# Attention and a two-layer MLP in one kernel: two batches share the second layer, with a second level of seven products, and the slots' small work is placed at 14 points

## The chip, the core and the metric

The kernel runs on one core of a Trainium2 chip. The core has five engines, each with its own in-order queue of instructions: TensorE (PE; its weight loads are shown apart as PEld), VectorE (DVE), ScalarE (ACT), GpSimd (POOL) and SyncE (SP, which issues the DMAs here). They wait for one another by semaphores only. The metric is the device time of one execution in microseconds.

## The reference: what is computed

For 8 batches of 12 heads, with 448 positions and a head size of 64, all in float32:

```python
q_n, k_n = rmsnorm(q, g_q), rmsnorm(k, g_k)
scores = q_n @ k_n.T / sqrt(64)
attn = softmax(scores) @ v
x = attn.transpose(0, 2, 1, 3).reshape(8 * 448, 768)
h = x @ w_in                 # 768 x 2048, float64 as given
out = (h - tanh(h)) @ w_out  # 2048 x 768
```

## The kernel before, in words

**Slots.** Attention is done for one pair of heads at a time. There are 48 such steps (8 batches of 6 pairs), numbered s = 0 to 47, and each has a slot in the instruction order, written by hand. Slots 0 to 5 are attention alone, with the rounding of the weights. In slots 6 to 11 the MLP of batch 0 runs beside the attention of batch 1. From slot 12 on, `slot` (the last of the three slot functions) does the values of step s, the scores of step s + 1 and the norms of step s + 2, and fills the rest with MLP matmuls.

**The MLP as a stream.** `mlp` is a generator that issues one matmul at a time: for each batch `hidden` (first layer and h - tanh h) and `project` (second layer). `run(ns)` draws matmuls from it until their estimated time is spent. `gap_ns` says how much MLP belongs to a slot: from slot 12 on four gaps of (H_NS + O_NS) / 24, drawn as eight halves, so that a batch's whole MLP is spread evenly over six slots. Whatever an evacuation or a sum of the MLP needs is issued by the generator at its place in the order, so it lands in the engines' queues between the attention's own work.

**Seven products.** From batch 1 on both layers are multiplied by a scheme of seven products of half-size blocks (`ORDER`: 1, 5, 6, 2, 3, 7, 4), instead of eight. For it, combinations of the weight blocks are made once and kept in DRAM (`w_in_dram`, `w_out_dram`); they are read back through a ring of six places, each load issued five products ahead (`ring_load`). Combinations of the moving side are made for each batch: `tt` from x in `divide` (lines 709 to 712, on POOL), and `tg` from g in `factors` and `rest` (lines 797 to 799 on DVE and POOL, 831 on POOL). A layer of a batch has 168 matmuls of 128x128 by 128x224: `hidden` has four sets of seven products of six matmuls, `project` three sets of seven products of eight. All are issued in line 750.

**Evacuation.** The products go to three PSUM banks named `mm` in turn; products 2, 3 and 7 are added on top of products 1, 5 and 6 in the same bank. DVE and ACT add them up in SBUF (`use`: lines 804 to 820 for the hidden layer, 867 to 881 for the second one). `shrink` (lines 786, 787) does tanh on ACT and the subtraction on DVE or POOL. Work put in `late["todo"]` is issued after the next product. `store` turns a 128x448 block on DVE (line 845) and issues four DMAs.

**A slot in its order.** First `visit`: 8 score matmuls of the last key chunk of step s + 1 (they read its kT and qT), then the values of step s mixed with the scores of s + 1, each exp on ACT. In it, `divide` copies one bank on ACT (line 687), adds the other on DVE (line 688, the "xT add") and multiplies by the reciprocal sums (line 692). Then come eight stretches of MLP matmuls with this work between them:

```python
add(s+1); square_blocks(s+2)                         # 552, 553; 466 on ACT
norm_blocks(s+2)          # 473, 475 to 477, and 478: pow on POOL
add_last(s+1); fold(s+1)                             # 560; 657, 659
scale_blocks(s+2); gather(s+1, 0)                    # 485; 667 on ACT
turn_blocks(s+2, 0); gather(s+1, 1)                  # 495: qT
turn_blocks(s+2, 1)                                  # 499: kT, 500 on ACT
spread_sums(s+1)                                     # 675 to 680
```

Lines 675 to 680 give the reciprocal sums that line 692 of the next visit multiplies by. The kT of step s + 2 is scaled on ACT (line 500) before the scores of the next visit read it.

Of the kernel before, what the change touches and what calls it, by code (L numbers as in the profile page):

```python
# [13 lines left out]
ALU = mybir.AluOpType  # L14
# [130 lines left out]
def bounded_path(tc, ctx, q, k, v, moe_w_in, moe_w_out, out, g_col, ident, ones, half_ones, neg_half, early):  # L145
# [32 lines left out]
    SETS = CF // 4  # L178
    ORDER = (1, 5, 6, 2, 3, 7, 4)
# [18 lines left out]
    gp = pool("gp", bufs=1)  # L198
    wp_stack = ctx.enter_context(ExitStack())
# [14 lines left out]

    def load(s, names):
        b, hp = steps[s]
        for name in names:
            src = {"q": q, "k": k, "v": v}[name]
            if s == 0 and name != "v":
                t = early[name]  # L220
            else:
                shape = [CP, 2, NCH, D] if name == "q" else [P, NCH, 2, D] if name == "k" else [P, 2, NCH, D]
                t = nat.tile(shape, F32, name=f"{name}_nat", bufs=3 if name == "v" else 2)
                fetch(nc, name, t, src[b, 2 * hp : 2 * hp + 2], in_order(s))
            loaded[name, s] = t
# [8 lines left out]
    BLOCKS = {1: 0, 2: 1, 4: 2, 7: 3, 5: 4, 6: 5, 3: 6}  # L234
    w_out_dram = scratch.tile([P, 7, HC, HF, P], F32, name="w_out")
# [140 lines left out]
    def ring_slot():  # L376
# [4 lines left out]
    ring_steps = [  # L381
        (b, layer, j, p)
        for b in range(1, B)
        for layer, count in ((0, SETS), (1, HC))
        for j in range(count)
        for p in ORDER
    ]
    ring_tiles = {}

    def ring_load(to):  # L390

        for n in range(len(ring_tiles), min(to, len(ring_steps))):
            b, layer, j, p = ring_steps[n]
            t = ring_tiles[ring_steps[n]] = ring_slot()
            if layer == 0:
                assert kept[1] > j
                nc.sync.dma_start(out=t[:, : 2 * HALF], in_=w_in_dram[j, p])
            else:
# [55 lines left out]
    def load_blocks(s):  # L454
        b, hp = steps[s]
        t = loaded["qk", s] = late["blocks"].tile([P, 2, NJ, BL], F32, name="qk_nat", bufs=2)
# [13 lines left out]
    def norm_blocks(s):  # L470

        mine, other = (late["blocks"].tile([P, 2 * NJ], F32, name=name, bufs=2) for name in ("rr_mine", "rr_other"))
        nc.vector.reduce_sum(mine, normed[s].rearrange("p i j d -> p (i j) d"), axis=AX.X)
        for g in range(P // BL):
            nc.vector.tensor_copy(out=other[g * BL : (g + 1) * BL], in_=mine[(g ^ 1) * BL : ((g ^ 1) + 1) * BL])
        nc.vector.tensor_tensor(out=mine, in0=mine, in1=other, op=ALU.add)
        nc.vector.tensor_scalar(out=mine, in0=mine, scalar1=1.0 / D, scalar2=1e-6, op0=ALU.mult, op1=ALU.add)  # L477
        nc.gpsimd.tensor_tensor(  # L478
            out=mine, in0=mine, in1=neg_half[:, :1].to_broadcast([P, 2 * NJ]), op=ALU.pow
        )  # L480
        normed["rr", s] = mine

    def scale_blocks(s):
        n, rr = normed[s], normed.pop(("rr", s))
# [59 lines left out]
    def add(s):  # L544
# [8 lines left out]
        nc.vector.tensor_tensor(out=t, in0=t, in1=p[2], op=ALU.add)  # L553
# [99 lines left out]
    def fold(s):  # L653

        t = sums.pop(s)[0].rearrange("p h s -> p (h s)")
        turned_sum = late["blocks"].tile([P, 2 * S], F32, name="sum_T")
        nc.vector.transpose(out=turned_sum, in_=t)
        part = late["blocks"].tile([P, 2 * NJ], F32, name="sum_32")
# [12 lines left out]
    def spread_sums(s):  # L671
# [5 lines left out]
        wide = late["blocks"].tile([2 * BL, NJ, BL], F32, name="sum_w")  # L677
        nc.vector.tensor_copy(out=wide, in_=total[:, :, None].to_broadcast([2 * BL, NJ, BL]))
        rs = whole[s] = late["blocks"].tile([2 * BL, S], F32, name="rs_T")
        nc.vector.transpose(out=rs, in_=wide.rearrange("p j k -> p (j k)"))  # L680

    def divide(s, av):
        b, hp = steps[s]
        rs = whole.pop(s)
        x = xT[b, hp] = xp.tile([P, S], F32, name="xT")
# [15 lines left out]
        if hp < HC:  # L701
            return
        c = hp - HC
        if c == 0:
            tt[b] = tp.tile([P, 3, HC, HS], F32, name="tt", bufs=1)
        eng = nc.vector if b == 0 and c == HC - 1 else nc.gpsimd
        x11, x12, x21, x22 = (xT[b, r][:, n : n + HS] for r in (c, hp) for n in (0, HS))
        t1, t2, t4 = (tt[b][:, i, c] for i in range(3))
        eng.tensor_tensor(out=t1, in0=x12, in1=x11, op=ALU.subtract)
        eng.tensor_tensor(out=t2, in0=x22, in1=t1, op=ALU.subtract)  # L710
        eng.tensor_tensor(out=x12, in0=x22, in1=x12, op=ALU.subtract)
        eng.tensor_tensor(out=t4, in0=x21, in1=t2, op=ALU.subtract)
# [16 lines left out]
    def products(b, layer, count, width, depth, moving, done_with):  # L729
# [8 lines left out]
        def product(j, p, bank, first):  # L738
# [20 lines left out]
            for fn in now:  # L759
                fn()  # L760

# [9 lines left out]
    def hidden(b):  # L771

        g = late["g"] = gp.tile([P, CF, S], F32, name="gT")
# [675 lines left out]
```

## Time and profile before

| what | value |
| --- | --- |
| median of 3 runs | 1391.6 us (1391.22 to 1391.68) |
| the profiled execution | 1391.42 us, of which its span is 1389.6 us |
| granted TensorE clock, mean | 0.992 |
| hidden layer and second layer, batches 1 to 7 (L750) | 2 records for each matmul, 352 to 354 ns each, overlapping |
| pow on POOL (L478) | 33 times, 4.84 us each |
| PE busy in the stretches of 100 us from 250 to 1250 us | 99.64 to 100.00 us |
| DMA | 249.91 MB, mean 180 GB/s |

The profile has a row for each instruction with its start and length. A group of rows has the same line of code, engine and operation; behind its busy time stands the idle time of the engine just before those instructions, and what ended it. Matmuls are pipelined, so the rate is read from the distance of starts over a stretch, not from the length of one row. In the order of time, a line gives the start, the length, the engine, the line of code, the operation with its output and inputs, and in brackets the idle time before it and what ended that.

### The profile page before, as it was taken

The numbers are of one execution on the slowest core, as the hardware profiler recorded it, in microseconds if no ns is written. First come the engines' busy times: TensorE is split into PE (matmuls) and PEld (weight loads), VectorE is DVE, ScalarE is ACT, GpSimd is POOL, SyncE is SP. The second block draws the span as 40 slices with busy tenths as digits, with TensorE's granted clock in tenths as the row PEclk, the third lists the DMA queues.
The fourth block names the chain that finished last, engine by engine and source line by source line (L and its number), as shares of the span: only waits on it lengthen the run. The fifth ranks groups of instructions, "written<-read, shape, count | busy, mean of one in ns | idle before, by whom it ended". The sixth has DMA issues, their size and how long they took to land.

```text
span 1389.6 us, 29917 instructions
## 1 busy us (share of the span) xinstructions
PE 1354.1 (97%) x11840; PEld 1128.4 (81%) x11840; DVE 941.0 (68%) x1545; ACT 504.7 (36%) x1147; POOL 561.8 (40%) x345
## 2 busy tenths in 40 slices
PE   7989899999999999999999999999999999999997
PEld 3458654478898898899889988988988998899997
DVE  4899888856876788567866668657875677633311
ACT  7856554234322433324332343324333234301100
POOL 4656565223642356225444236323552354402310
PEclk9999999999999999999999999999999999999999
DMA  7888778766666666666657666666567667366663
GB/s 170 187 218 240 249 232 222 206 181 170 177 181 160 177 172 165 176 170 181 178 152 195 177 156 188 172 162 183 165 167 176 181 173 189 100 189 184 191 194 90
DMA packets 367657, 249.91 MB, mean 180 GB/s; under 512 B 281748, under 2 KB 309780, under 8 KB 367508
## 3 DMA queue, kind: packets, MB, share of 16 engines
q1 hardware_dynamic: 367504, 247.90, 66.5%
q8 instruction: 96, 1.57, 0.5%
q14 instruction: 53, 0.43, 0.1%
q10 hardware_dynamic: 4, 0.00, 0.0%
HBM read 214.40 MB, written 33.42 MB: 178 GB/s over the span
## 4 chain that ended last, share of the span: by engine, by line
PE 85%; DMA 6%; DVE 4%; SPq 2%; ACT 1%; issue 1%; POOL 1%; ACTq 0%; DVEq 0%; POOLq 0%
PE mm L750 65%; PE sc L521 8%; PE sc L582 6%; PE mm L915 4%; DMA w_raw<-in_moe_w_in_dram 2%; DMA w_f<-w_out 1%; PE sc L570 1%; DMA gT<-in_moe_w_in_dram 1%; DMA w_raw<-in_moe_w_out_dram 1%; DMA k_nat<-in_k_dram 1%; SPq L272 1%; DVE w_out L82 1%; DVE w_out L79 1%; PE sc L620 1%; DVE w_out L335 0%
## 5 line engine op out<-in xcount | busy, mean ns | idle before, releaser
L750 PE MATMUL mm<-xT,w_f 128*128 128x224 f32 x1392 | 278.5, 354 | 1.7 <-DVE s L806 1.7
L750 PEld LDWEIGHTS mm<-xT,w_f 128*128 128x128 f32 x1392 | 261.3, 190 | 16.0 <-issue 10.2
L750 PEld LDWEIGHTS mm<-gT,w_f 128*128 128x128 f32 x1344 | 252.8, 190 | 12.8 <-issue 12.8
L750 PE MATMUL mm<-gT,w_f 128*128 128x224 f32 x1344 | 263.0, 354 | 0.0
L478 POOL TENSOR_TENSOR rr_mine<-rr_mine,neg_half 128x28 f32<-128x28 f32 x33 | 159.7, 4839 | 218.2 <-DVE rr_mine L477 218.2
L521 PE MATMUL sc<-qT,kT 64*32 64x448 f32 (+1 forms) x3072 | 217.4, 503 | 10.0 <-ACT p_last L527 9.0
L750 PE MATMUL mm<-tt,w_f 128*128 128x224 f32 x1044 | 208.7, 353 | 0.0
L750 PEld LDWEIGHTS mm<-tt,w_f 128*128 128x128 f32 x1044 | 197.0, 190 | 4.4 <-issue 4.4
L787 POOL TENSOR_TENSOR gT<-s,th 128x448 f32<-128x448 f32 x96 | 120.4, 1262 | 197.0 <-ACT th L786 188.2
L750 PE MATMUL mm<-tg,w_f 128*128 128x224 f32 x1008 | 197.5, 352 | 0.0
L750 PEld LDWEIGHTS mm<-tg,w_f 128*128 128x128 f32 x1008 | 190.7, 190 | 0.0
L521 PEld LDWEIGHTS sc<-qT,kT 64*32 64x32 f32 x3072 | 71.1, 107 | 78.5 <-issue 56.2
L688 DVE TENSOR_TENSOR xT<-xT,sc 128x448 f32<-128x448 f32 x35 | 21.7, 621 | 166.5 <-PE sc L521 110.8
L710 POOL TENSOR_TENSOR tt<-xT,tt 128x224 f32<-128x224 f32 x23 | 31.1, 1353 | 234.2 <-DVE xT L692 212.0
L667 ACT COPY sum_g<-sum 32x14 f32<-32x14 f32 x280 | 56.3, 201 | 186.2 <-DVE sum L659 180.5
L582 PE MATMUL sc<-p,v_nat 64*32 64x448 f32 x1120 | 110.5, 536 | 0.0
L786 ACT ACTIVATE th<-s 128x448 f32<-128x448 f32 x96 | 55.2, 575 | 112.7 <-DVE s L812 59.8
L527 ACT ACTIVATE p<-sc 128x448 f32<-128x448 f32 x132 | 71.7, 543 | 51.7 <-PE sc L521 39.1
L915 PE MATMUL mm<-gT,w_out 128*128 128x448 f32 x192 | 75.9, 551 | 0.2 <-POOL w_out L90 0.2
L915 PEld LDWEIGHTS mm<-gT,w_out 128*128 128x128 f32 x192 | 36.3, 193 | 38.3 <-issue 35.8
L582 PEld LDWEIGHTS sc<-p,v_nat 64*32 64x32 f32 x1120 | 40.6, 107 | 31.0 <-issue 31.0
L142 POOL TENSOR_TENSOR rr<-rr,neg_half 112x8 f32<-112x8 f32 (+1 forms) x30 | 49.0, 1660 | 33.7 <-DVE rr L141 33.6
(151 smaller groups left out, 1828.3 us busy)
## 6 DMA issues: line engine op xcount, KB each, us to landing
w_f<-w_in SPq DMA_DIRECT2D x196, 384.0 KB, 3.3
w_f<-w_out SPq DMA_DIRECT2D x147, 512.0 KB, 4.2
w_raw<-in_moe_w_out_dram SPq DMA_DIRECT2D x16, 768.0 KB, 5.2
out_dram<-th SPq DMA_DIRECT2D x192, 56.0 KB, 1.9
w_in<-w_out SPq DMA_DIRECT2D x21, 384.0 KB, 5.9
qk_nat<-in_q_dram SPq DMA_DIRECT2D x132, 56.0 KB, 2.5
qk_nat<-in_k_dram SPq DMA_DIRECT2D x132, 56.0 KB, 2.6
v_nat<-in_v_dram SPq DMA_DIRECT2D x72, 96.0 KB, 3.7
```

Of the source, the lines that this page charges most:

```text
L142: nc.gpsimd.tensor_tensor(out=r, in0=r, in1=neg_half[:rows], op=ALU.pow)
L478: nc.gpsimd.tensor_tensor(out=mine, in0=mine, in1=neg_half[:, :1].to_broadcast([P, 2 * NJ]), op=ALU.pow)
L521: nc.tensor.matmul(tiles[h][i * BL : (i + 1) * BL, :n], lhsT=kT[r, c * P + at : c * P + at + BL], rhs=qT[r, first : first + n], start=True ...
L527: nc.scalar.activation(p[:, h, c if c < 2 else 0, :], tiles[h][:, :n], AF.Exp, scale=1.0 if rr is None else rr[:, 0, 2 * c + h : 2 * c + h ...
L582: nc.tensor.matmul(av[g][i * BL : (i + 1) * BL, :S], lhsT=v_nat[keys, h, c, m * BL : (m + 1) * BL], rhs=p[keys, h], start=first, stop=True ...
L667: nc.scalar.copy(out=acc[h * BL : (h + 1) * BL, g], in_=part[g * BL : (g + 1) * BL, h * NJ : (h + 1) * NJ])
L688: nc.vector.tensor_tensor(out=x, in0=x, in1=av[1][:, :S], op=ALU.add)
L710: eng.tensor_tensor(out=t2, in0=x22, in1=t1, op=ALU.subtract)
L750: nc.tensor.matmul(bank[:, f * HS : (f + 1) * HS], lhsT=w[:, c * width + f, :], rhs=moving[p](c), start=(first and f == 0 and c == 0), sto ...
L786: nc.scalar.activation(th, h, AF.Tanh, bias=0.0, scale=1.0)
L787: eng.tensor_tensor(out=g[:, rows, cols], in0=h, in1=th, op=ALU.subtract)
L915: nc.tensor.matmul(bank[:, :S], lhsT=w_out_row(f, n // HC)[:, n % HC * P : (n % HC + 1) * P], rhs=g[:, f, :], start=(f == 0), stop=(f == C ...
```

## The change

- **Two batches share a second layer.** Batches 0 and 1 stay as they are. From batch 2 on the order is `hidden(b)`, `hidden(b + 1)`, `project_pair(b)`. The pair's second layer is one product of 2048 x 896 (both batches' columns side by side), done by seven outer products whose operands are g of one or the other batch, or sums of both, made in place (`outer_sum`). Each outer product has three blocks of 128 rows. One of them is done plainly by eight matmuls of 448 columns; the other two by a second level of seven products of four matmuls of 224 columns each.
- **Inner sums.** The moving side of the inner products is four sums of 128x896 per outer one (`inner_sum`, buffers `u`), made on POOL one outer product ahead (the first four on DVE).
- **Inner weights.** The combinations of weight blocks for the second level are made once, from the kept outer ones, beside the MLP of batch 1 (`inner_steps`): 14 loads of 512 KB, 28 sums of 128x512 on POOL, 35 stores. One step of it is issued after each product.
- **Combining.** `combine_outer` adds the outer products into two accumulators or into an output block, and stores it.
- **The x sums** (`x_sums`, formerly in `divide`) are issued from batch 2 on at the end of the layer before, all on POOL.
- **`factors` and `tg`** exist for batch 1 only.
- **The slots' work** is put at 14 points at equal distances, in smaller pieces. The reciprocal sums (points 12 and 13) and the turn of kT (point 14, the last) now end the slot.
- **How much MLP a slot holds**: slots 12 to 19 share batch 1's MLP (8 slots); after that, of each twelve slots, eight hold two hidden layers and four hold the paired second layer. The last four slots hold the hidden layer of batch 6; that of batch 7 and the last paired layer follow without attention.

The diff, cut to its core:

```diff
     def hidden(b):
...
+        if b < PAIRED or b % 2 == 0:
+            g = gp.tile([P, CF, S], F32, name="gT")
+        else:
+            g = late["second"].tile([P, CF, S], F32, name="g2")
...
     def divide(s, av):
...
-        eng.tensor_tensor(out=t1, in0=x12, in1=x11, op=ALU.subtract)
...
+        if b < PAIRED and hp >= HC:
+            x_sums(b, (c,), range(4), nc.vector if b == 0 and c == HC - 1 else nc.gpsimd)
...
+    def inner_steps():
...
+            for n, (out, x, y, op) in enumerate(work):
+                yield lambda: nc.gpsimd.tensor_tensor(out=out, in0=x, in1=y, op=op)
+                if n == 0 and i + 1 < len(OUTER):
+                    fetch_outer(i + 1)
+            keep(i, 0, a11)
+            keep(i, 1, block(sums, 0, 2))
+            keep(i, 3, a12)
+            keep(i, 4, block(sums, 2, 2))
+            keep(i, 6, a22)
+            yield lambda: None
...
+    def project_pair(b):
...
+        outer_plan = {
+            3: {0: [(0, 0, V), (0, 1, V), (1, 0, G)], 5: [(0, 2, V), (1, 1, G)], 2: [(0, 3, V)],
+                3: [(1, 2, V)], 4: [(1, 3, V)]},
+            2: {0: [(2, 0, V), (2, 1, V)], 1: [(2, 2, V)], 5: [(2, 3, V)]},
+            6: {1: [(3, 0, G)], 2: [(3, 1, G)]},
+            7: {1: [(3, 2, G)], 2: [(3, 3, G)]},
+        }
+        inner_plan = {5: 0, 6: 1, 7: 2, 4: 3}
+        for i in range(4):
+            inner_sum(OUTER[0], i, V)
...
+        def combine_outer(p, m, y):
+            e, f = acc[:, m], acc2[:, m]
...
+            if p == 2:
+                add(o, y, e)
+                store(b, m, o)
+            elif p == 6:
+                add(e, e, y)
+                add(f, f, e)
+            elif p == 7:
+                add(e, e, y)
+            elif p == 5:
+                add(f, f, y)
+                add(o, y, e)
+                store(b + 1, m, f)
+                store(b + 1, HC + m, o)
+            else:
+                add(o, y, e)
+                store(b, HC + m, o)
...
+        for k, p in enumerate(OUTER):
...
+            bank = mm_bank()
+            yield from matmuls(bank, S, lambda i: w[:, i], [rows(p, f, 1, slice(0, S))[:, 0] for f in range(HF)], True)
+            flush()
+            at(k, 0)
+            late["todo"].append(lambda p=p, v=bank[:, :S]: combine_outer(p, HC - 1, v))
...
+            for i, q in enumerate(ORDER):
...
+                first = q not in (2, 3, 7)
+                bank = banks[q] = mm_bank() if first else banks[{2: 1, 3: 5, 7: 6}[q]]
...
+                yield from matmuls(bank, HS, lambda c: w[:, c], moving, first)
+                flush()
...
+                at(k, q)
...
-        return (H_NS + O_NS) / (4 * NP)
+        if s < 2 * NP + 8:
+            return (H_NS + O_NS + AHEAD_NS) / 32
+        return (H_NS if (s - 2 * NP - 8) % 12 < 8 else PAIR_NS) / 16
...
+        work = (
+            ((following, lambda: add(s + 1, False)), (blocks, lambda: square_blocks(s + 2))),
+            ((following, lambda: add_third(s + 1)),),
+            ((blocks, lambda: norm_blocks(s + 2)), (not blocks, turn_rows)),
+            (
+                (blocks, lambda: meet_blocks(s + 2)), (ahead, lambda: squares(s + 3)),
+                (has(s + 4) and not by_blocks(s + 4), lambda: load(s + 4, "qk")),
+            ),
+            ((following, lambda: add_last(s + 1)), (blocks, lambda: power_blocks(s + 2))),
+            ((folded, lambda: fold(s + 1)),),
+            ((folded, lambda: fold_rest(s + 1)),),
+            ((ahead, lambda: norm(s + 3)), (folded, lambda: gather(s + 1, 0))),
+            ((blocks, lambda: scale_blocks(s + 2)),),
+            ((folded, lambda: gather(s + 1, 1)),),
+            ((blocks, lambda: turn_blocks(s + 2, 0)), (ahead, lambda: norm_q(s + 3))),
+            ((folded, lambda: spread_sums(s + 1)),),
+            ((folded, lambda: turn_sums(s + 1)),),
+            ((blocks, lambda: turn_blocks(s + 2, 1)), (s + 3 == TURNED, lambda: load_blocks(s + 3))),
+        )
+        for point in work:
+            run(4 * gap / (len(work) + 1))
...
```

## The prediction

> **What bounds the kernel now.** I read the busy table first, then the stretches, then the order of time of one slot.
>
> ```profile
> span 1389.6 us, 29917 instructions
> PE 1354.1 (97%) x11840; PEld 1128.4 (81%) x11840; DVE 941.0 (68%) x1545; ACT 504.7 (36%) x1147; POOL 561.8 (40%) x345
> ```
>
> PE is busy 97% of the span. From 250 to 1250 us the stretches of 100 us show 99.6 to 100 us of PE in each, at a granted clock of 1.00. So fewer matmuls help only as far as no other engine is late. The chain of waits repeats one slot (one head pair of attention): 112 records of L750 in 21.38 us. A 128x128 by 128x224 f32 matmul is two records, so one costs 21.38/56 = 0.3818 us. Slots start 26.81 us apart (1128.21 to 1155.00 for one of them), so the attention matmuls of a slot, its **visit**, cost 26.81 - 21.38 = 5.43 us.
>
> DVE at 68% looks free. It isn't: this is VectorE's order of time in one slot whose MLP part is hidden layer.
>
> ```profile
> 1128.21 0.62 DVE L688 TENSOR_TENSOR xT<-xT,sc 128x448 f32<-128x448 f32 x1 [5.48 <-ACT xT L687]
> 1128.87 1.25 DVE L692 TENSOR_TENSOR xT<-xT,rs_T 64x448 f32<-64x448 f32 x2
> ...
> 1135.32 0.19 DVE L476 TENSOR_TENSOR rr_mine<-rr_mine,rr_other 128x28 f32<-128x28 f32 x1
> 1135.55 0.18 DVE L477 TENSOR_SCALAR rr_mine<-rr_mine 128x28 f32<-128x28 f32 x1
> 1135.64 0.62 DVE L816 TENSOR_TENSOR s<-mm,s 128x448 f32<-128x448 f32 x1
> 1136.17 1.26 DVE L560 TENSOR_TENSOR rows<-rows,p_last 64x448 f32<-64x448 f32 x2
> ...
> 1141.41 1.23 DVE L485 TENSOR_TENSOR qk_n<-qk_nat,rr_mine 128x896 f32<-128x896 f32 x1
> 1142.56 1.55 DVE L797 TENSOR_TENSOR tg<-gT 128x448 f32<-128x448 f32 x1
> 1144.22 1.37 DVE L798 TENSOR_TENSOR tg<-gT,tg 128x448 f32<-128x448 f32 x1
> 1145.51 0.63 DVE L495 STREAM_TRANSPOSE qT<-qk_n 128x448 f32<-128x448 f32 x1
> 1146.07 0.58 DVE L806 TENSOR_TENSOR s<-mm,s 128x448 f32<-128x448 f32 x1
> 1146.58 0.62 DVE L499 STREAM_TRANSPOSE kT<-qk_n 128x448 f32<-128x448 f32 x1
> ...
> 1149.14 0.58 DVE L787 TENSOR_TENSOR gT<-mm,th 128x448 f32<-128x448 f32 x1
> 1155.00 0.62 DVE L688 TENSOR_TENSOR xT<-xT,sc 128x448 f32<-128x448 f32 x1 [5.28 <-PE sc L521]
> ```
>
> From the first xT add at 1128.21 to 1149.72 DVE never waits: 21.5 us. Then it sits idle until the next xT add, because its next instruction needs the end of the visit; over the kernel L688 has 166.5 us of idle before it in 35 slots, 4.75 us each. 21.5 + 5.3 is the whole 26.8 us. So a hidden-layer slot is already full on DVE as well as on PE. It costs nothing so far because kT (the last thing that the next visit needs) is turned at 1146.58, with 3 us of other DVE work behind it; ACT scales it from 1147.23 to 1147.90, and the visit begins at 1155.00 - 5.48 = 1149.5.
>
> **The change on PE.** By the listing of both kernels' instruction order, attention and batch 0 keep their matmuls. Second layers of batches 1 to 7 fall from 1176 matmuls of 224 columns to 168 (batch 1) + 588 narrow ones + 168 of 448 columns. A wide one costs two narrow ones: 16 of L915 run from 271.65 to 283.87, 12.22/16 = 0.764 us. So 1176 - (168 + 588 + 336) = 84 units less: 84 x 0.3818 = **32.1 us** gained, if nothing is late. The rest goes by the new division of a slot: 42 units in the slots over hidden layers (20 to 27, 32 to 39, 44 to 47), 77 in the four over a paired second layer (28 to 31, 40 to 43), 42.75 in 12 to 19. PE alone then needs 42 x 0.3818 + 5.43 = 21.47, 34.83 and 21.75 us.
>
> **The new loop.** In the changed order the DVE transposes of the sums (point 13) and of kT (point 14) come last in a slot, and DVE's next instruction after kT is the xT add of the next visit. PE's first score matmul of that visit waits for ACT's kT. So a slot can't be shorter than: visit start to xT add, 5.48 (880.52 to 886.00 in one slot), + all DVE work of the slot, + kT on ACT 0.67 and two hand-overs of 0.04 and about 0.1 (the first read at 875.65 to 875.69, the second an estimate): 5.48 + W + 0.8.
>
> W in a hidden-layer slot. Take the 21.5 us above; L797 and L798 leave (2.95, 1142.56 to 1145.51); seven evacuations of 448 columns instead of nine (0.54 from start to start): 21.5 - 2.95 - 1.08 = 17.5. The second way is from the groups' means. Attention: 1.10 + 1.38 + 2 x 0.64 + 1.06 + 4 x 0.25 + 0.19 + 0.18 + 1.43 + 0.64 + 0.63 + 1.11 + 1.09 + 0.23 + 0.23 + 0.48 + 0.64 + 0.62 + 2 x 0.62 = 14.5; evacuations 7 x 0.61 = 4.3; 18.8, less 0.6 since PSUM adds overlap their forerunner by 0.07. One wait may add: pow on POOL ends 4.89 us after L477 (731.64 to 736.53), and the work now between them is 4.6, so 0.3. W is 17.5 to 18.8; I take 18.2, between a slot with quick two-input adds and the means. The slot becomes 5.48 + 18.2 + 0.8 = 24.5 against PE's 21.47: **3.0 us of new PE stall** where there was none.
>
> Slot by slot, DVE work up to kT from the same means less 0.6:
> - Fourteen plain ones (20-22, 24-26, 32-34, 36-38, 44, 45): 14 x 3.0 = 42.
> - 27 and 39 also hold the four first inner sums (128x896, two SBUF inputs, no such row; as L552 to L553, 1.1 to 1.38 each): W 23.7, 30.0 - 21.47 = 8.5 each, 17.
> - 23 and 35: nine POOL sums of the next batch's x (0.66 or 1.5 us, L709, L710) lie ahead of pow and delay DVE's scaling: 3.0 + 2, twice, 10. Slot 19: 1.5.
> - 13 to 15 still hold batch 1's factors: W 19.2, 19.8, 21.5: 3.8 + 4.4 + 6.1. 17 to 19: W 17.2, 1.7 each. 16: none. Together 19.5.
> - Paired slots: W is 22.5, 28.6, 22.7, 29.9 against 34.83 - 6.3 = 28.5, so only the last is over (1.4). But a bank now has to come free within four matmuls (1.53 us). Following slot 29 in its order: its combine of the 448-wide product lies behind two outer sums and ends some 1.1 us late, the evacuations of products 5 and 6 follow 0.4 and 1.2 late: 2.7. I take 5 per phase of four, 10, and 2 in the last pair, which has no attention beside it.
> - Inner weights, made beside batch 1: 28 POOL sums of 512 (128x448 takes 1.135, L787, so 1.3) and 49 DMAs more on SP's in-order queue, whose stores wait for POOL and whose loads wait for stores. Pow queues behind these sums. No row shows it: 0 if POOL is idle then, up to 16 if every second pow is held 4 us (the landing time of 384 to 512 KB loads, 3.3 to 4.2). I take 5. Behind the stores on SP stand ring loads, five products (11 us) ahead of need.
>
> Stalls: 42 + 17 + 10 + 1.5 + 19.5 + 12 + 5 = 107. Net: -32 + 107 = +75. The profiled execution took 1391.42 (span 1389.6 and 1.8 around it; the median of the runs is 1391.6, the same within 0.2). 1391.4 + 75 = **1466 us**. With W 17.5, no hold by DMA and 4 for the paired slots the stalls are 69 (1428); with W 18.8, 16 there and 30 in the paired slots 153 (1512).
>
> What goes at nothing: ring traffic (a second layer drops from 2 x 21 loads to 35 smaller ones per pair), stores (the same 192), the last store (two adds and a transpose behind the last matmul, 0.7 longer).
>
> On POOL and DVE together the trace shows the same add of 128x896 (L485) at 1.09, mostly 1.54 and up to 2.01 us, and L710 at 0.66 or 1.50. The Trainium skill (SBUF — State Buffer, "Who interferes with whom") says why such times jump: a VectorE instruction with two SBUF inputs and a GpSimd instruction that reads SBUF exclude each other for a whole instruction. It speaks against moving 30 sums per pair to POOL: held up once by each, DVE would lose some 30 x 2.2 us, an estimate by that rule, about 130 us more for the two phases with attention than I count.
>
> **Rivals.**
> 1. *The saving arrives* (faster). One mechanism: the finer points let DVE work through a hidden slot in 21.47 - 6.3 = 15.2 us, so kT is never late; then 1391.4 - 32 + 2 to 4 = 1361 to 1364. For it: the factors and their POOL partners are gone and two-input adds get quicker. Against: the quietest slot of the trace needs 17.5 for the same list.
> 2. *Milder*: W near 17 and clean paired slots, 14 x 1.8 = 25 and 35 elsewhere: 1395 to 1428.
> 3. *POOL becomes the bound*: a paired phase has 30 sums of 896 (2.25 us by 2 x L787's 1.135, 3.0 by L799's 1.52), 4 pows of 4.8 and 12 x sums, 95 to 122 us of 145; slot 29 alone has ten sums, 27 to 35 us of 35. If u sums come late, PE waits 10 us or more a phase: 1512 to 1560.
> 4. *It doesn't do what it says*: excluded nearly, the listing counts the matmuls.
>
> **How the numbers follow.** The DVE loop 0.74; milder 0.08; POOL 0.09; faster 0.07; no change (stalls eat just the gain) 0.02. A change of under 0.2% is about what a measurement of this kernel can't tell from none. Faster 0.07, same 0.02, slower 0.91. The main case alone is 1428 to 1512; half of either neighbour brings the range to 1415 to 1520.
>
> **What would show it.** Right: PE idle of some 3 us once per hidden slot ahead of the scores, released by ACT's kT; slots 24 to 25 us apart there; DVE idle only before the xT add; paired slots 35 to 37.5 us apart; L1023 with 84 units less. Wrong: PE at 99% in those slots with a distance of 21.5 us (rival 1); matmuls that wait for POOL's u (rival 3); pow that waits for DMAs beyond 5 us in all.

## The result, and the profile after

The changed kernel takes 1512.4 us (median of 4 runs, 1511.27 to 1515.54) against 1391.55 (4 runs of the kernel before): 1.088 times as long, 95% interval 1.086 to 1.089. That is 121 us more; 75 were predicted, with 1520 as the upper end of the range.

The page's first part, for the changed kernel:

```profile
span 1511.1 us, 29074 instructions
PE 1358.7 (90%) x11336; PEld 1046.7 (69%) x11336; DVE 1049.5 (69%) x1620; ACT 509.1 (34%) x1159; POOL 735.9 (49%) x415
```

PE has 504 records fewer, two for each matmul: 252 matmuls less. That is the count of the prediction (924 in the second layers of batches 1 to 7 instead of 1176, 168 of them wide; a wide one counted twice, 84 units less). Yet PE's busy time grew by 4.6 us, and its share fell from 97% to 90%. Two things hide in that: idle time, and matmuls that run longer. The list of waits of PE (us in total, times, longest) opens with a row that the kernel before doesn't have:

```profile
PE sc L552 <- ACT kT L531: 85.0, 27, 6.8
```

Here is a plain hidden-layer slot, DVE's order of time with ACT's kT and PE's first score matmul put in. It answers to the slot from 1128.21 to 1155.00 of before.

```profile
515.50 0.62 DVE L736 TENSOR_TENSOR xT<-xT,sc 128x448 f32<-128x448 f32 x1 [8.03 <-PE sc L552]
516.16 1.27 DVE L740 TENSOR_TENSOR xT<-xT,rs_T 64x448 f32<-64x448 f32 x2
...
528.05 1.09 DVE L516 TENSOR_TENSOR qk_n<-qk_nat,rr_mine 128x896 f32<-128x896 f32 x1 [0.85 <-POOL rr_mine L509]
...
532.26 0.62 DVE L725 STREAM_TRANSPOSE rs_T<-sum_w 64x448 f32<-64x448 f32 x1
532.82 0.59 DVE L530 STREAM_TRANSPOSE kT<-qk_n 128x448 f32<-128x448 f32 x1
...
533.45 0.67 ACT L531 ACTIVATE kT<-kT,g_col 128x448 f32<-128x448 f32 x1 [3.10 <-DVE kT L530]
...
534.17 0.61 PE L552 MATMUL sc<-qT,kT 64*32 64x224 f32 x16 [2.65 <-ACT kT L531]
...
539.67 0.62 DVE L736 TENSOR_TENSOR xT<-xT,sc 128x448 f32<-128x448 f32 x1 [6.25 <-PE sc L552]
```

The loop closes as predicted: DVE works without a pause (but for 0.85 us for pow) up to kT, ACT scales kT, PE waits 2.65 us for it, and the next xT add comes 6.25 us after kT. The slot is 24.17 us, where PE alone needs 21.47 by the prediction's count: 17.91 from the xT add to the end of kT (the prediction's W was 18.2), and 6.26 from there to the next xT add.

The distances of the xT adds give the account slot by slot. "Over PE" is the sum of the slots less what PE alone needs (21.47, 21.75 in slots 13 to 19, 34.83 in paired ones).

| slots | distances, us | over PE | predicted |
| --- | --- | --- | --- |
| 14 plain ones | 24.11 to 24.28 | 38 | 42 |
| 27, 39 | 30.53, 30.61 | 18 | 17 |
| 23, 35 | 29.17, 29.24 | 15 | 10 |
| 13 to 19 | 31.19, 33.69, 34.54, 27.23, 24.83, 23.89, 26.73 | 50 | 21, and 5 for the inner weights |
| 28 to 31, 40 to 43 | 37.68, 41.63, 35.51, 42.03; the same within 0.1 | 35 | 10 |

Together 157; less the 32.1 gained on PE, 125, against 121 measured. (The last pair, predicted at 2, has no xT adds to read.) So the named loop is there in its named size. Against the prediction's terms, slots 13 to 19 are 24 us more, the paired ones 25 and slots 23 and 35 5, and the plain ones 4 less: these make up the missing 46 us, but for a few.

**A slow stretch behind the long waits.** In the plain slots the time from the end of kT to the next xT add is 6.2 to 6.3 us. In nine others (13 to 16, 19, 23, 27, 35, 39) it is 8.0 to 9.2, 21 us more in all (they lie within the table's rows), though the same instructions stand there. Slot 23: PE's wait, and busy times by stretch (the span of the stretch, its length, then the busy time of PE, PEld, DVE, ACT and POOL, each with its number of instructions; the number behind POOL's is the granted clock, ahead of the DMA share and GB/s):

```profile
608.83 1.00 PE L552 MATMUL sc<-qT,kT 64*32 64x224 f32 x16 [3.62 <-ACT kT L531]
```

```profile
600.00:605.00 5.00, 4.60 (x24) 4.46 (x24) 4.15 (x7) 2.75 (x10) 3.82 (x2) 1.00 0.55 137
608.83:611.00 2.17, 2.17 (x32) 0.89 (x40) 0.00 (x0) 1.44 (x4) 1.14 (x1) 0.50 0.79 177
611.00:614.00 3.00, 3.00 (x40) 0.88 (x32) 0.00 (x0) 0.54 (x1) 0.00 (x0) 0.50 0.39 155
614.00:615.00 1.00, 1.00 (x24) 0.35 (x16) 0.00 (x0) 0.54 (x1) 0.00 (x0) 0.66 0.00 0
615.00:617.00 2.00, 2.00 (x56) 0.71 (x40) 0.00 (x0) 1.33 (x3) 0.00 (x0) 1.00 0.00 0
```

After 3.62 us without a matmul the clock is 0.50 for over 5 us: the first 16 score matmuls take 1.00 us where those of the plain slot above took 0.61, behind a wait of 2.65. In this run the clock fell behind each wait for kT of 3.28 us or more (the nine slots) and behind none of 2.91 or less, and each of the nine cost 1.7 to 3 us beyond the wait itself. In few_sums (below) it fell behind two of 2.61 and 2.64 us as well (slots 24 and 36, 1.7 us longer than the other plain ones), so the length of the wait alone doesn't decide.

The Trainium skill (TensorE: Matmul & The Clock Gate, Part 1) puts the idle time after which the clock is halved at about 3.4 us, and the busy time that brings it back at the same. The 2.65 and 3.62 us agree with the first; the 3.28, and the 2.61 and 2.64 of few_sums, don't. In slot 23 the clock was back at 1.00 only 5.2 to 6.2 us after PE's restart.

### The profile page after: what moved, and what is told of

Read it like the earlier page. It is cut to its first block, busy times and chain, and to the rows that moved or that the text cites. A ratio compares the mean times of both kernels' runs of the same rounds, so it can differ in the third digit from the quotient of the medians.

```text
span 1511.1 us, 29074 instructions
## 1 busy us (share of the span) xinstructions
PE 1358.7 (90%) x11336; PEld 1046.7 (69%) x11336; DVE 1049.5 (69%) x1620; ACT 509.1 (34%) x1159; POOL 735.9 (49%) x415
## 4 chain that ended last, share of the span: by engine, by line
PE 47%; DVE 25%; POOL 12%; issue 6%; DMA 3%; ACT 3%; SPq 2%; DVEq 0%; ACTq 0%; POOLq 0%
PE mm L1023 18%; POOL rr_mine L509 9%; PE mm L804 9%; PE sc L552 8%; PE sc L618 5%; PE mm L1173 4%; DVE qk_n L516 2%; DVE rows L589 2%; DVE rr_other L501 2%; DVE rows L583 2%; DVE xT L740 1%; DMA w_raw<-in_moe_w_in_dram 1%; DVE rr_mine L494 1%; ACT kT L531 1%; POOL g L949 1%
## 5 line engine op out<-in xcount | busy, mean ns | idle before, releaser
L804 PE MATMUL mm<-xT,w_f 128*128 128x224 f32 x1104 | 224.2, 357 | 7.7 <-DMA w_f<-w_in 3.3
L804 PEld LDWEIGHTS mm<-xT,w_f 128*128 128x128 f32 x1104 | 209.8, 192 | 14.9 <-issue 5.9
L804 PEld LDWEIGHTS mm<-tt,w_f 128*128 128x128 f32 x1044 | 196.3, 191 | 17.3 <-issue 12.8
L1023 PE MATMUL mm<-u,w_f 128*128 128x224 f32 x672 | 142.4, 364 | 20.4 <-issue 9.6
L1023 PEld LDWEIGHTS mm<-u,w_f 128*128 128x128 f32 x672 | 129.5, 195 | 26.9 <-issue 16.4
L1023 PE MATMUL mm<-gT,w_f 128*128 128x224 f32 (+1 forms) x480 | 135.6, 437 | 0.8 <-DVE s L1030 0.8
L736 DVE TENSOR_TENSOR xT<-xT,sc 128x448 f32<-128x448 f32 x26 | 16.2, 622 | 169.9 <-PE sc L552 109.8
L849 POOL TENSOR_TENSOR gT<-s,th 128x448 f32<-128x448 f32 x60 | 73.0, 1218 | 105.5 <-ACT th L848 101.9
L1023 PEld LDWEIGHTS mm<-gT,w_f 128*128 128x128 f32 x480 | 93.9, 197 | 40.3 <-issue 37.5
L1023 PE MATMUL mm<-g,w_f 128*128 128x224 f32 (+1 forms) x360 | 98.1, 428 | 0.0
L849 POOL TENSOR_TENSOR g<-s,th 128x448 f32<-128x448 f32 x36 | 41.9, 1164 | 112.0 <-ACT th L848 111.3
L1023 PEld LDWEIGHTS mm<-g,w_f 128*128 128x128 f32 x360 | 68.1, 190 | 28.2 <-issue 28.2
```

What stands on the lines that cost most here:

```text
L804: nc.tensor.matmul(bank[:, f * HS : (f + 1) * HS], lhsT=w[:, c * width + f, :], rhs=moving[p](c), start=(first and f == 0 and c == 0), sto ...
L849: eng.tensor_tensor(out=g[:, rows, cols], in0=h, in1=th, op=ALU.subtract)
L1023: nc.tensor.matmul(bank[:, :n], lhsT=w(i), rhs=mv, start=(first and i == 0), stop=(i == len(moving) - 1), skip_group_check=not first,)
```

## The experiments

Theory after the result: (1) the loop through DVE and kT makes all of the loss outside the paired slots; (2) what the prediction sized too small is DVE's time wherever POOL makes sums at the same time, and the halved clock behind long waits. Rivals: for (1), VectorE's amount of work wherever kT stands, or the 14 points as such; for (2), the order of VectorE's queue, one PSUM bank, the uneven division of the MLP over the slots, or POOL as the bound. All runs were taken in rounds beside the kernel before (1390.2 to 1390.7 us there). less_dve, few_sums and no_inner_sums leave out work and don't compute the reference's result.

| run | us | times the kernel before, 95% interval |
| --- | --- | --- |
| the change itself | 1512.4 | 1.088 (1.086 to 1.089) |
| kt_first | 1422.3 | 1.023 (1.022 to 1.025) |
| less_dve | 1472.8 | 1.058 (1.054 to 1.063) |
| points_only | 1404.1 | 1.009 (1.007 to 1.011) |
| few_sums | 1497.6 | 1.077 (1.075 to 1.079) |
| act_wide | 1422.9 | 1.025 (1.023 to 1.028) |
| half_beat | 1425.3 | 1.026 (1.024 to 1.028) |
| half_beat_even | 1450.6 | 1.043 (1.042 to 1.045) |
| even_kt_first | 1450.8 | 1.044 (1.043 to 1.046) |
| no_inner_sums | 1401.8 | 1.010 (1.007 to 1.012) |
| sums_on_dve | 1422.5 | 1.024 (1.022 to 1.025) |
| sums_on_pool | 1432.0 | 1.031 (1.029 to 1.033) |
| dve_wide_first | 1412.1 | 1.015 (1.013 to 1.017) |

### Is it the place of kT? kt_first

```diff
+            ((blocks, lambda: turn_blocks(s + 2, 1)), (s + 3 == TURNED, lambda: load_blocks(s + 3))),
             ((folded, lambda: spread_sums(s + 1)),),
             ((folded, lambda: turn_sums(s + 1)),),
-            ((blocks, lambda: turn_blocks(s + 2, 1)), (s + 3 == TURNED, lambda: load_blocks(s + 3))),
```

> The changed kernel with one thing moved: the turn of kT goes ahead of the reciprocal sums (point 12 instead of 14; the sums go to points 13 and 14). The work is the same. Theory (the loop visit, DVE work up to kT, ACT's kT): 1.6 us of sums and one evacuation of 0.54 leave the stretch up to kT, so the plain hidden-layer slots fall from 24.2 to about 22.1 us (14 of them, -29), the others by 1.5 to 2 each, and where PE waits short enough the half clock after it goes too: in all 1430 to 1455 us. Rival 1 (POOL sets the pace: pow, inner sums): the order on DVE is of no matter, 1495 to 1512. Rival 2 (DVE's throughput alone, wherever the work stands): 1505 to 1515.

1422.3 us: one line moved by two points takes back 90 of the 121 us, more than expected. In PE's waits, the row of after with 85.0 us becomes:

```profile
PE sc L552 <- ACT kT L531: 17.7, 23, 1.9
```

The longest wait left there is 1.9 us, and the halved clock behind kT goes too: the time from kT's end to the next xT add is 6.2 to 6.5 us in all of slots 13 to 26. Plain slots are 22.05 us apart, slots 13 to 19 172.4 us together instead of 202.1, slots 23 and 35 24.2, 27 and 39 22.7. The paired ones hardly answer: 154.5 us instead of 156.9. Outside them the 122 us over PE become 37, of which 17.7 are still waits for kT. So theory (1) stands for most of that loss, and the paired slots have another cause.

### Or VectorE's amount of work? less_dve

```diff
-            ((following, lambda: add_third(s + 1)),),
+            ((following and s < 13, lambda: add_third(s + 1)),),
...
-        nc.vector.tensor_tensor(out=t, in0=p[0], in1=p[1], op=ALU.add)
+        if s < 14:
+            nc.vector.tensor_tensor(out=t, in0=p[0], in1=p[1], op=ALU.add)
```

> The changed kernel without the two DVE adds of the probabilities of 128x896 (from step 14 on; the sums of the softmax are then wrong): 2.5 us of DVE work less in each slot, nothing else changed. Theory (DVE loop): plain slots from 24.2 to 21.7 us, just above PE's 21.47, the slots with batch 1 and the paired ones shorter by 2 to 3 us too, in all 1415 to 1445 us. Rival 1 (POOL sets the pace): 1490 to 1512. If only the paired slots do not answer (under 1 us each), it is POOL that holds those, and the time is near 1440.

1472.8 us, a miss: 40 us gained instead of 67 to 97. A plain slot (but for slot 32, 0.4) loses 0.7 to 0.8 us of the 2.2 that the two adds took. DVE's order of time in one (lines from L583 on stand one further down):

```profile
497.01 0.62 DVE L871 TENSOR_TENSOR s<-mm,s 128x448 f32<-128x448 f32 x1 [0.51 <-PE mm L805]
497.55 1.07 DVE L494 TENSOR_REDUCE rr_mine<-qk_n 128x28 f32<-128x896 f32 x1
499.28 0.62 DVE L873 TENSOR_TENSOR s<-mm,s 128x448 f32<-128x448 f32 x1 [0.65 <-PE mm L805]
...
506.31 1.09 DVE L516 TENSOR_TENSOR qk_n<-qk_nat,rr_mine 128x896 f32<-128x896 f32 x1 [0.85 <-POOL rr_mine L509]
```

Where DVE has nothing to do it now waits in its queue for products (0.51, 0.65), and pow is still awaited for 0.85: the loop has a second strand, from the square's sum (L494) through pow, beside the bare sum of DVE's work. In a plain slot the amount of work counts for about a third of what is taken away.

### Or the 14 points as such? points_only

The kernel before, with the slots' work in the changed kernel's list of 14 points (its functions cut into the same pieces), the last of which are:

```diff
+            ((folded, lambda: spread_sums(s + 1)),),
+            ((folded, lambda: turn_sums(s + 1)),),
+            ((blocks, lambda: turn_blocks(s + 2, 1)), (s + 3 == TURNED, lambda: load_blocks(s + 3))),
+        )
+        for point in work:
+            run(4 * gap / (len(work) + 1))
```

> The kernel before with only its slots' work put at the 14 points; no shared second layer, no inner weights. Theory (kT last closes the loop): a hidden-layer slot has 21.5 us of DVE work, and 21.5 + 6.3 = 27.8 against PE's 26.8, in half of the 34 slots: 1398 to 1412 us, slower than the kernel before. Rival (the finer points are a gain by themselves, or of no matter where PE is the bound): 1385 to 1393 us.

1404.1 us, as expected: 13.9 us, a ninth of the loss. PE waits for kT for 15.5 us, in 17 slots; kT ends 20.1 to 22.5 us after the xT add instead of 16.2 to 19.0, but a slot of before holds 56 matmuls, and 26.8 us leave room for most of that. The new order is dear only together with the short slots.

### Why slots 13 to 16 are so long: few_sums, half_beat

few_sums leaves out the inner weights' POOL sums of six of the seven outer blocks:

```diff
-                yield lambda: nc.gpsimd.tensor_tensor(out=out, in0=x, in1=y, op=op)
+                yield (lambda: nc.gpsimd.tensor_tensor(out=out, in0=x, in1=y, op=op)) if i == 0 else (lambda: None)
```

> The changed kernel with the POOL sums of the inner weights made for the first of seven outer blocks only (the other six blocks keep the first's sums, so the second layers of batches 2 to 7 are wrong); all loads and stores of the inner weights stay. In the changed kernel the slots 13 to 16 take 31.2, 33.7, 34.5 and 27.2 us where 25.5, 26.1, 27.8 and 21.8 were expected. Theory (pow stands behind those sums on POOL, and DVE's two-input adds meet them): these slots fall to 26 to 29 us, 1485 to 1497 in all. Rival (the DMAs of the inner weights: the busier DMA engines, ring loads behind stores on SP): no change, 1507 to 1515.

1497.6 us, 0.6 outside the theory's span. Slots 13 to 16 lose 2.1, 3.0, 2.8 and 4.9 us: POOL's sums lengthen them, but at 29.1, 30.7, 31.8 and 22.4 us three of the four stay above the 26 to 29 expected: these sums are about a third of what the four slots are over PE (12.8 of 39.7 us). How POOL lengthens them is seen in slot 15 of the changed kernel:

```profile
394.20 4.58 POOL L949 TENSOR_TENSOR g<-g 128x512 f32<-128x512 f32 x3
...
394.26 2.15 DVE L516 TENSOR_TENSOR qk_n<-qk_nat,rr_mine 128x896 f32<-128x896 f32 x1 [0.73 <-POOL rr_mine L509]
```

and the same instruction in few_sums, with no sum beside it:

```profile
391.41 1.09 DVE L516 TENSOR_TENSOR qk_n<-qk_nat,rr_mine 128x896 f32<-128x896 f32 x1 [0.72 <-POOL rr_mine L509]
```

So 14.8 us by the medians for 24 sums (12.8 in slots 13 to 19 of the two traces), where the prediction had 5 for all 28 and looked for it in pow's delay by DMAs: over the kernel, sums L949 wait 2.1 us for DMAs.

half_beat (on top of act_wide, below) issues an inner-weight step after every second product only:

```diff
-                inner_step()
+                late["beat"] = late.get("beat", 0) + 1
+                if late["beat"] % 2:
+                    inner_step()
```

> As act_wide, and a step of the inner weights' making is issued only after every second product, so that it spreads from batch 1 over the hidden layer of batch 2. Theory (POOL's 28 sums and what waits behind them lengthen slots 13 to 16): these four slots lose 1 to 3 us each against kt_first's 25.8, 27.8, 27.1 and 23.9, and the slots from 17 on gain less than 1 each: 4 to 10 us below act_wide. Rival (what lengthens them is batch 1's own sums on VectorE, the factors, and not the inner weights): within 2 us of act_wide, or above it.

1425.3 against act_wide's 1422.9: the theory missed. Nine of the 28 sums now lie in slots 20 to 23. Slots 13 to 19 fall by 0.9 us together; 20 to 23 rise by 4.7 (23.1 to 23.3 instead of 22.05 in the plain ones). The steps weren't cheaper in those slots, but dearer: about 0.5 us for each sum that moved there.

### The paired slots: a bank, or the division? act_wide, even_kt_first, half_beat_even

act_wide is kt_first with ACT taking the wide product out of its bank:

```diff
             e, f = acc[:, m], acc2[:, m]
+            if p not in (1, 3) and m == HC - 1:
+                o = part("s1").rearrange("p f s -> p (f s)")
+                nc.scalar.copy(out=o, in_=y)
+                y = o
```

> Base is the run with kT's turn at point 12 (kt_first: 1422.3 us; its paired slots 28 to 31 are 35.25, 41.72, 35.5 and 42.04 us apart, where TensorE alone needs 34.8). Added here: ACT copies the 448-wide outer product of five of the seven outer products out of its PSUM bank, and VectorE adds from the copy. Theory (the bank of the wide product comes free late, because its add stands behind other two-input adds on VectorE, and TensorE stands still and then runs at a lower clock): the second and fourth paired slot fall to 36 to 39 us, together 6 to 11 us per phase, the whole to 1400 to 1412 us. Rival (VectorE or POOL as a whole is too slow in these slots): they stay at 41 to 42 us, the whole at 1418 to 1427 us.

1422.9: the rival holds for the whole time (slots 29 and 31 came to 43.20 and 39.91 us). The wide bank comes free early, and a narrow product's bank takes its place. It is released by a DVE add (L1030) that ends an unbroken stretch of DVE work from the slot's start on, 4.94 us of it an L740 beside two POOL sums (slot 29; the same L740 is shown for kt_first below):

```profile
713.76 1.05 DVE L990 TENSOR_TENSOR g<-g,gT 128x896 f32<-128x896 f32 x1
714.73 1.26 DVE L596 TENSOR_TENSOR rows<-rows,p_last 64x448 f32<-64x448 f32 x2
716.02 0.39 DVE L1030 TENSOR_TENSOR s<-mm,s 128x224 f32<-128x224 f32 x1
...
716.46 2.86 PE L1023 MATMUL mm<-gT,w_f 128*128 128x224 f32 x8 [4.01 <-DVE s L1030]
```

even_kt_first is kt_first with the same amount of MLP in every slot from 24 on; half_beat_even is half_beat with the same edit:

```diff
-        return (H_NS if (s - 2 * NP - 8) % 12 < 8 else PAIR_NS) / 16
+        if s < 4 * NP:
+            return H_NS / 16
+        return (2 * H_NS + PAIR_NS) / 48
```

> kt_first (1422.3 us) with the even division alone: from slot 24 on 53.7 units of MLP in each slot; VectorE still empties the wide product's bank. Theory as in half_beat_even: 1398 to 1412 us. If only the late banks matter and not the slot's length, 1416 to 1428 us.

> As half_beat, and from slot 24 on every slot holds the same amount of MLP (53.7 units instead of 42 in eight slots and 77 in four of each twelve). TensorE needs 53.7 x 0.3818 + 5.43 = 25.9 us a slot then. Theory (a hidden-layer slot is short for TensorE, 21.5 us, against VectorE's unchanged list; a longer slot gives VectorE room): slots 24 to 43 end within 1 us of 25.9, the whole 8 to 20 us below half_beat. Rival (the slots with the paired layer are bound by their banks, not by the slot's length): the slots that hold the paired layer stay 2 us or more above 25.9, the whole within 6 us of half_beat.

1450.8 and 1450.6, on the wrong side by 28 and 25 us; both theories missed. Slots with hidden layer alone came to 25.65 to 26.13, as PE needs them. But the paired layer now stretches over slots 27 to 32, and these take 191.4 us where PE needs 155.4: 36 over, instead of 15 for kt_first's four. PE waits 23.9 us ahead of L1023 in these six slots, and 10.2 in kt_first's slots 27 to 32. Each slot brings one attention list for DVE, whatever its MLP, so that six such lists instead of four stand beside the paired layer's sums. That this is the cause is argued, not shown: over slots 24 to 33 DVE is busy 227.4 us and POOL 147.5, against 227.5 and 151.8 in kt_first (537 units of MLP there instead of 560), so neither engine is busier as a whole. Slot 28 of even_kt_first shows how a bank comes late:

```profile
688.30 4.89 POOL L990 TENSOR_TENSOR g<-g 128x896 f32<-128x896 f32 x2 [9.00 <-DVE gT L990]
...
690.25 5.21 DVE L501 COPY rr_other<-rr_mine 32x28 f32<-32x28 f32 x4
...
693.15 2.07 POOL L997 TENSOR_TENSOR u<-gT 128x896 f32<-128x896 f32 x1
...
696.25 3.19 PE L1023 MATMUL mm<-g,w_f 128*128 128x224 f32 x8 [4.83 <-DVE acc L1030]
```

Four tiny copies that take 0.74 us elsewhere last 5.21, till the POOL sums beside them are done; PE stands 4.83 us for the add behind them, and its next eight records take 3.19 us, where eight take 1.78 after a wait of 2.26.

### Exclusion between VectorE and POOL, or VectorE's own list? no_inner_sums, sums_on_dve, sums_on_pool

Three edits of kt_first. no_inner_sums leaves out POOL's sums `u` from the second outer product on; the other two put the paired layer's sums on one engine:

```diff
+            if p != OUTER[0]:
+                us[p, i] = us["kept", i]
+                return
```

```diff
-        V, G = nc.vector, nc.gpsimd
+        V = G = nc.vector
```

in sums_on_dve (the x sums stay on POOL), and `V = G = nc.gpsimd` in sums_on_pool, where the first four inner sums stay on VectorE. By the plan in the code each paired layer has six outer sums on POOL and ten on VectorE; the expectations below say five and eleven.

> Base is kt_first (1422.3 us; paired slots 28 to 31 take 35.25, 41.72, 35.5 and 42.04, together 154.5 us, against 139.3 for TensorE alone). In each paired layer POOL's sums u for the second level are left out from the second outer product on (24 sums of 128x896; the first product's four are used again), so the output is not the reference's. VectorE's work is unchanged. Theory (POOL's sums hold back VectorE's instructions with two inputs in SBUF, which last 2 to 2.9 us there instead of 1.05): the four slots fall to 141 to 147 us together, the whole to 1398 to 1412 us. Rival (VectorE's own list and its order make the bank late): they stay at 152 to 155 us, the whole at 1416 to 1424.

> kt_first with all sums of the paired layer on VectorE: 24 inner and 5 outer ones of 128x896 more per layer, 29 x 1.05 = 30 us more work for VectorE in the four paired slots, and as much less for POOL at 2.1 to 2.5 each. If exclusion between the two engines is most of the loss, the extra work is paid by quicker instructions: four slots 150 to 160 us together, the whole 1415 to 1435. If VectorE's amount of work sets these slots: 172 to 185 us, the whole 1455 to 1490.

> kt_first with all sums of the paired layer but the first four on POOL: 11 outer ones leave VectorE (11 x 1.05 = 11.6 us per layer) and take POOL 11 x 2.1 to 2.5. If VectorE's own list and its order (outer sums ahead of the emptying of banks) make the banks late: four slots 140 to 147 us, the whole 1395 to 1410. If exclusion is most of it, the gain is eaten: 150 to 160 us, the whole 1415 to 1435; if POOL itself becomes the bound, matmuls wait for u and it is above that.

All three came out inside the spans of the exclusion theory: 1401.8, 1422.5 and 1432.0 us; slots 28 to 31 take 144.6, 155.0 and 159.2 together. These are the sums over the four slots (length, then busy time of PE, PEld, DVE, ACT, POOL), of kt_first:

```profile
sum 154.51, PE 144.29 PEld 108.52 DVE 123.66 ACT 35.72 POOL 102.18; mean PE 36.07 PEld 27.13 DVE 30.91 ACT 8.93 POOL 25.54
```

of no_inner_sums:

```profile
sum 144.58, PE 140.97 PEld 106.16 DVE 98.13 ACT 35.71 POOL 45.36; mean PE 35.24 PEld 26.54 DVE 24.53 ACT 8.93 POOL 11.34
```

and of sums_on_dve:

```profile
sum 154.95, PE 143.91 PEld 108.01 DVE 124.24 ACT 35.75 POOL 32.27; mean PE 35.98 PEld 27.00 DVE 31.06 ACT 8.94 POOL 8.07
```

DVE's instructions are the same in the first two, but POOL's 24 sums make them 25.5 us longer (123.66 - 98.13), 1.06 us a sum. With those sums and POOL's six outer ones made on DVE, at 1.08 us each, DVE is busy 124.24 - 98.13 = 26.1 longer. **Beside a full DVE, a sum on POOL took about as much of DVE as making it there, and over 2 us of POOL besides.** The single instructions say how. Slot 29 of kt_first, DVE and POOL in the order of time:

```profile
699.33 2.09 POOL L997 TENSOR_TENSOR u<-gT 128x896 f32<-128x896 f32 x1 [1.72 <-PE mm L1023]
...
699.38 4.93 DVE L740 TENSOR_TENSOR xT_more<-xT_more,rs_T 64x448 f32<-64x448 f32 x2
...
701.38 2.46 POOL L997 TENSOR_TENSOR u<-gT,u 128x896 f32<-128x896 f32 x1
...
711.03 5.56 POOL L509 TENSOR_TENSOR rr_mine<-rr_mine,neg_half 128x28 f32<-128x28 f32 x1 [7.20 <-DVE rr_mine L503]
...
714.12 1.05 DVE L990 TENSOR_TENSOR g<-g,gT 128x896 f32<-128x896 f32 x1
...
716.56 2.07 POOL L997 TENSOR_TENSOR u<-g 128x896 f32<-128x896 f32 x1
...
716.69 2.89 DVE L990 TENSOR_TENSOR g<-g,gT 128x896 f32<-128x896 f32 x1
```

The same L990 takes 1.05 us beside pow and 2.89 beside a sum that started 0.13 us before it; L740 takes 4.93 instead of 1.27 and ends when two sums are done. In sums_on_dve the rows of L990 (min, median, max in ns) show no such spread:

```profile
L990 DVE TENSOR_TENSOR gT<-g,gT x12: 1076/1082/1083, 680.6 to 1322.9; 128x896 f32<-128x896 f32 x12
L990 DVE TENSOR_TENSOR g<-g,gT x12: 1047/1081/1121, 707.2 to 1335.2; 128x896 f32<-128x896 f32 x12
```

against kt_first's

```profile
L990 DVE TENSOR_TENSOR gT<-g,gT x12: 1075/1542/2966, 682.7 to 1321.9; 128x896 f32<-128x896 f32 x12
L990 DVE TENSOR_TENSOR g<-g,gT x12: 1048/1084/2890, 710.9 to 1335.6; 128x896 f32<-128x896 f32 x12
```

What no_inner_sums has left over PE, 144.6 - 139.3 = 5, lies in slots 31 (36.37 us) and 29 (39.47), the latter the slot in which the prediction had found evacuations late by following the order. In slot 29 an L990 still lasts 2.89 us, beside one of POOL's outer sums that started 0.14 us before it, and PE waits 2.33 us for a bank.

In sums_on_pool the longest wait of PE is 9.37 us, put down to no engine ("issue"). It isn't a wait for `u`: it ends 0.10 us after a DVE add that empties a wide bank, and that add stands behind four copies held till POOL's sums are done (slot 29):

```profile
712.51 7.01 DVE L501 COPY rr_other<-rr_mine 32x28 f32<-32x28 f32 x4
713.38 6.12 POOL L990 TENSOR_TENSOR g<-g,gT 128x896 f32<-128x896 f32 x3
...
719.88 0.62 DVE L1030 TENSOR_TENSOR s<-mm,acc 128x448 f32<-128x448 f32 x1
...
720.60 3.33 PE L1023 MATMUL mm<-u,w_f 128*128 128x224 f32 x8 [9.37 <-issue]
```

### What is left with all sums on VectorE: dve_wide_first

```diff
             flush()
+            combine_outer(p, HC - 1, bank[:, :S])
             at(k, 0)
-            late["todo"].append(lambda p=p, v=bank[:, :S]: combine_outer(p, HC - 1, v))
```

> sums_on_dve (1422.5 us; paired slots 34.1, 38.9, 39.3 and 42.6, together 155 us) with one edit: VectorE's add that takes the 448-wide outer product out of its bank is issued as soon as its matmuls are, ahead of the sums that stand at the same place, instead of after the next inner product. In sums_on_dve TensorE stands still for 1.9, 2.8 and 4.4 us ahead of three such banks in slots 29 to 31 and then runs 3 us at half the clock. Theory (this place in VectorE's queue is what remains): four slots 142 to 148 us together, the whole 1398 to 1410 us. Rival (VectorE's backlog as a whole makes all banks late, in whatever order): 150 to 156 us, the whole 1413 to 1424. By either it stays above the kernel before (1390.3).

1412.1 us, between the two: the four slots take 148.5 us in the first phase and 151.5 in the second. The wide bank's place in the queue was worth 9 of the some 30 us that these slots were still over PE (10 by the medians). Of the rest, 10.9 us are six waits for banks of narrow products and 7.6 four waits for banks of wide ones. Of the versions with the shared second layer that compute everything, this is the fastest, and it is still 1.5% over the kernel before. No version that was run beats that kernel, no_inner_sums with its work left out included.

## Why the prediction was right, and where it was short

- **The sign, the mechanism and the units: right.** 84 units fewer, a loop of kT's turn, ACT and the next visit, and idle time of PE just ahead of the scores. kt_first is the proof: one moved line, 90 us. Most of what the prediction asked to see came: 24 to 25 us between plain slots (24.2), PE idle for 2.65 us ahead of the scores, DVE idle only ahead of the xT add but for 0.85 us at pow. Paired slots 35 to 37.5 us apart didn't: they took 35.5 to 42.1.
- **The time: inside the range, in part by luck.** The main case reached 1512 only with W at 18.8, 16 us for the inner weights and 30 for the paired slots. The last two turned out near that; W didn't (17.9), and 21 us came from the halved clock, which has no term in the sum.
- **W: right where POOL is quiet.** 17.9 us for 18.2 in plain slots, 20.0 for 20.2 in slots 23 and 35. In slots 27 and 39 the distance came out (30.5 for 30.0) by two errors that cancel: W was 22.0 instead of 23.7, and the visit 2.2 us longer. Beside the inner weights' sums W was too small: 23.2, 24.5, 25.7 and 19.2 us in slots 13 to 16, where 19.2, 19.8 and 21.5 and, for slot 16, no wait were predicted. Its term for pow was 0.3 and measured 0.85, and less_dve shows that this strand is next in line.
- **Visit: too short behind long waits.** The 5.48 us was held fixed. In nine slots the stretch from kT to the xT add took 1.7 to 3 us more at half the clock, 21 us in all, as much as nearly half of the missing 46; the kernel before has no such wait for kT, and no price was put on one.
- **Inner weights: mis-sized.** 5 us, thought to come through pow and DMAs; 13 to 15 measured for 24 of the 28 sums. What the traces show beside them is DVE's instructions taking longer (2.15 us for 1.09).
- **Paired slots: mis-sized, for a stated reason.** 5 a phase, 17.5 measured. Here the prediction weighed the skill's rule on VectorE and GpSimd (SBUF — State Buffer, "Who interferes with whom"), which would have added about 130 us for both phases, and counted none of it. By kt_first and no_inner_sums DVE lost 25.5 us a phase to the 24 inner sums, 51 for both, of which about 10 a phase reached the end (154.5 to 144.6). So the rule was right in kind for these sums, at under half the estimate; beside pow, which reads SBUF on POOL too, DVE's adds of 128x896 kept 1.05 to 1.12 us.
- **The plain slots at a minus of 4** and the paired ones' PE time (34.09 us in slot 28 of no_inner_sums, where PE never waits, against 34.83) took a little back.
- **Rivals.** The saving arrives: no. Milder: no. POOL as the bound: the time lies at the lower end of its span, but not by its mechanism; POOL is busy 102 of 154.5 us in kt_first's paired slots, and matmuls that wait for `u` weren't found. PE's waits ahead of L1023 put down to no engine are 9.6 us in the changed kernel and 20.7 in sums_on_pool, six in each; all of these end 0.10 us after a DVE add L1030.

What stays open: how the 50 us over PE in slots 13 to 19 divide. 10.7 of them are the longer way from kT to the xT add in slots 13 to 16 and 19. kt_first takes 30 of the 50, few_sums 13, but the two overlap, since a shorter wait can also spare the halved clock; both together weren't tried. Batch 1's own sums on POOL (L861, L895) stand beside DVE adds of 1.84 to 2.02 us in those slots; they weren't taken away.

## What to carry to other kernels

When two engines' lists meet once per step, write the loop as a sum (from the step's start to the last thing that the next step needs, plus the hand-over) and look at which instruction stands last: moving the one that is awaited ahead of two that aren't was worth 90 of 121 us. A sum on POOL isn't free for DVE: price it at DVE's own time for it as well, unless the DVE work beside it is seen to keep its length. An even division isn't a gain by itself: here it stretched the paired layer over six slots instead of four, with late banks in more of them, and lost 28 us.

## What the runs showed of the hardware

- In the changed kernel PE's clock was granted at 0.50 for over 5 us after a wait of 3.62 us, and stayed at 1.00 after waits for kT of up to 2.91; in few_sums it was 0.50 behind waits of 2.61 and 2.64 us.
- DVE adds with two inputs in SBUF lasted up to 2.97 us instead of 1.08 beside POOL's sums of 128x896 (kt_first), and four copies of 32x28 5.21 (even_kt_first) and 7.01 us (sums_on_pool) instead of 0.74; beside pow, DVE's adds of 128x896 kept 1.05 to 1.12 (kt_first, four of them).
